# A decode step on one core: the last two rows of one weight matrix loaded in eight partition pieces, and repeated waits left out

## The chip, the cores and the metric

The kernel runs on one core of one Trainium2 chip. The metric is the device time of one execution in microseconds (us). Times come as the median of several runs; one more execution was taken with the hardware profiler, and all rows of the profile belong to that one.

## The reference

One token (a row of 1024 numbers) goes through an attention block over a long cache and through a small network beside it; the results are added. All inputs are bf16.

```
xn  = layernorm(A_x)                                     # 1 x 1024
q   = xn @ wq                                            # 32 heads of 128
o   = softmax(q k^T / sqrt(128)) v                       # 4 cached heads, 65536 positions each; 8 query heads share one
A   = o @ wo                                             # wo: 4096 x 1024
h   = gelu(layernorm(xn) @ w1), shifted by positions     # one position, so the shifts leave zeros
x1  = xn + h @ w2
B   = x1 + gelu(layernorm(x1) @ w3) @ w4                 # w3: 1024 x 3584, w4: 3584 x 1024
out = A_x + A + B
```

The caches are 2 x 4 x 65536 x 128 bf16, 128 MiB in all, and the weights about 36 MB; each byte is read once.

## The kernel before

Work is written out by hand into five queues, one for each engine (class `_Q`). A queue is a list of operations and of waits on semaphores; `emit` writes it out in that order, and the order in the list is the order on the engine. `_B` objects stand for buffers. Each keeps the events that wrote it (`w`) and those that read it (`r`) as a table from semaphore to value. Ahead of an operation, `_deps` puts a wait into the queue for every event that the buffers ask for; `_Q.wait` leaves out a wait whose value the same queue has already waited for. After it, `_done` records the operation's own event: `set_write` replaces the buffer's events, `add_write` (with `partial=True`) adds to them. TensorE's queue is rolled into a loop of eight passes of four tiles each (`emit_looped`), whose waits take their values from registers.

All large loads are issued by SyncE (SP), in one queue `q_sp`, through `_dma`. Each load has a semaphore of its own (`chan(name)`), which rises by 16 when the load has landed.

The stages are these. First `wq` (8 MB) and the first cache pieces are loaded, and the query is computed. Then come 32 tiles of 8192 positions (`NT`), the main loop. Each 4 MB load of keys or values serves two tiles; it goes into one of two slots of `KV`, and SP issues it when the readers of that slot (VectorE's transposes at L488 for keys, TensorE's products at L546 for values) are done with it. In the loop the tile's keys are transposed (L488), multiplied with the query (L499), turned into exponentials (L529), transposed back (L539), multiplied with the values (L546) and accumulated (L558, L560).

Late in the loop SP issues the loads of `w1`, `w2` and `w3`, then `wo` (8 MB, L629) into `KV`, then `w4` into the tile `WX`. `w4` is seen as 128 partitions of 28 rows; one row of one partition is 1024 bf16, 2 KB. It is loaded in three pieces of 20, 6 and 2 rows (`w4_parts`, L630), all 128 partitions at once, into column ranges of `WX` that do not overlap. Each piece has its own buffer object `b_W4[i]`, whose `r` is filled by hand at L632 to L636 with all earlier uses of that memory:

```
        w4_parts = [(0, 20), (20, 6), (26, 2)]
        b_W4 = [_B() for _ in w4_parts]
```

The last piece is 128 x 2 rows, so 4 KB for each partition and 512 KB in all. After the main loop TensorE does the products with `w1`, `w2`, `w3` (helper line L459) and with `wo` and `w4` (helper line L447). `w4_pe(i)` waits for piece i and issues four matmuls for each of its rows: 80, 24 and 8 of them. After the last eight VectorE copies the result out of PSUM (L664), and SP stores it, four partitions of 256 bf16 (L665); SP waits for that store, and the program ends.

Of the kernel before, what the change touches and what calls it, by code (L numbers as in the profile page):

```python
# [13 lines left out]
class _Q:  # L14
    def __init__(self, name, sem, in_order=False):
        self.name = name
        self.sem = sem
        self.in_order = in_order
        self.ops = []
        self.cnt = 0  # L20
        self.waited = {}
        self.marks = []
# [75 lines left out]
class _B:  # L98

    def __init__(self, name=""):  # L100
        self.name = name
        self.w = {}
        self.r = {}

    def set_write(self, ev):
        self.w = {ev[0]: ev[1]}
        self.r = {}

    def add_write(self, ev):
        self.w[ev[0]] = max(self.w.get(ev[0], 0), ev[1])  # L110

    def add_read(self, ev):
# [1 line left out]


def _deps(q, reads, writes):
    for b in reads:
        for s, v in b.w.items():
            q.wait((s, v))
    for b in writes:  # L120
        for s, v in list(b.w.items()) + list(b.r.items()):
            if not (q.in_order and s is q.sem):
                q.wait((s, v))


def _done(ev, reads, writes, partial=False):
    for b in reads:
        b.add_read(ev)
    for b in writes:
        if partial:  # L130
            b.add_write(ev)
        else:
            b.set_write(ev)


def _op(q, fn, reads=(), writes=(), partial=False):
    _deps(q, reads, writes)
    ev = q.op(fn, True)
    _done(ev, reads, writes, partial)
    return ev  # L140


def _grp(q, fns, reads=(), writes=(), partial=False):
    _deps(q, reads, writes)
    ev = None
    for i, fn in enumerate(fns):
        ev = q.op(fn, i == len(fns) - 1)
    _done(ev, reads, writes, partial)
    return ev
# [8 lines left out]
def _dma(q, chan, fn, reads=(), writes=(), partial=False):  # L158
    _deps(q, reads, writes)
    chan.n += 1  # L160
    ev = q.dma(fn, chan.sem, 16 * chan.n)
    _done(ev, reads, writes, partial)
    return ev


def bass_parallel_sum__gqa_block_cached__mixer_s_mlp__decode_kernel(
# [13 lines left out]
    P = 128  # L180
    D = A_x.shape[2]
# [15 lines left out]
    with ExitStack() as es:  # L197
        E = es.enter_context

        def sb(name, shape, dt):  # L200
            return E(nc.sbuf_tensor(name, shape, dt))
# [4 lines left out]
        def sem(name):  # L206
            return E(nc.semaphore(name))
# [52 lines left out]
        WX = sb("WX", [P, 14336 + 16384], BF)  # L260
# [23 lines left out]
        q_sp = _Q("sp", None)  # L284
# [3 lines left out]
        def chan(name):  # L288
            if name not in chans:
                chans[name] = _DmaChan(sem("d_" + name))  # L290
            return chans[name]
# [26 lines left out]
        def load_rows(dst, bufs, ch, w, r0, nrow):  # L318
            src = w.rearrange("(p r) n -> p (r n)", p=P)
            ncol = w.shape[1]  # L320
            _dma(q_sp, chan(ch), lambda e: e.dma_start(out=dst, in_=src[:, r0 * ncol:(r0 + nrow) * ncol]), writes=bufs)
# [309 lines left out]
        b_W4 = [_B() for _ in w4_parts]  # L631
        for i, (r0, nr) in enumerate(w4_parts):  # L632
            for b in [b_W, b_W2] + b_X[0] + b_X[1]:
                for d in (b.r, b.w):
                    for s, v in d.items():
                        b_W4[i].add_read((s, v))  # L636
            load_rows(WX[:, r0 * D:(r0 + nr) * D], [b_W4[i]], "w4%d" % i, B_w4, r0, nr)

        def w4_pe(i):
            r0, nr = w4_parts[i]  # L640
# [60 lines left out]
```

## Time and profile before

| | |
|---|---|
| median of 3 runs | 402.36 us (402.34 to 403.08) |
| the profiled execution's own time | 402.32 us |
| its span, first to last instruction | 401.1 us |
| outside the span | 1.2 us |
| moved from HBM | 169.87 MB, 424 GB/s over the span |
| busy: PE, DVE, ACT, POOL | 41%, 58%, 12%, 19% of the span |

The DMA engines (16 of them serve the core) are busy nearly all of the span; no compute engine is above 58%. The chain that ended last puts 64% of the span on DMA. SP issues the three pieces of `w4` at 349.97 to 351.25 us; their times from issue to landing are 43.7, 46.9 and 47.6 us. The last eight matmuls start at 398.51 us, and the result's store is issued at 399.40 us.

### The profile page before, as it was taken

Reading aid. Unit: us, or ns where it says so; the run is one execution under the profiler, and the core shown is the slowest. Engines: PE = TensorE matmul, PEld = TensorE weight load, DVE = VectorE, ACT = ScalarE, POOL = GpSimd, SP = SyncE. Lnnn points to the kernel's source line nnn. Section 1 sums busy time; section 2 is a strip of 40 time slices with the busy share of each in tenths; the row PEclk is TensorE's granted clock in tenths of the full one; section 3 lists DMA queues with packets and bytes.
Section 4 is the critical chain, followed back from the end, with each engine's and each line's share of the span. In section 5 each row is a group of like instructions: output and inputs, shape, how many; then the busy total and the mean of one; then the engine's idle time right before and its main releaser. Section 6 shows DMA issues by size and latency. Waiting matters only on the chain.

```text
span 401.1 us, 4292 instructions
## 1 busy us (share of the span) xinstructions
PE 165.6 (41%) x1544; PEld 53.3 (13%) x1560; DVE 231.8 (58%) x398; ACT 49.5 (12%) x132; POOL 77.1 (19%) x130
## 2 busy tenths in 40 slices
PE   0432325353443434343434343524353535536054
PEld 0211101011111111110111110101010101222032
DVE  0246566757575858585758585848585857354000
ACT  1000101111111111110202111111111112100000
POOL 5000003121223121112412121214112111420000
PEclk9985556556556565565565565565655655757567
DMA  8999999999999999999999999999999999999994
GB/s 356 428 418 435 446 422 422 451 433 418 431 449 428 422 448 432 425 428 444 431 422 448 435 425 428 444 429 422 451 431 425 428 448 408 473 443 440 414 395 181
DMA packets 6070, 170.03 MB, mean 424 GB/s; under 512 B 804, under 2 KB 808, under 8 KB 936
## 3 DMA queue, kind: packets, MB, share of 16 engines
q1 hardware_dynamic: 5912, 169.87, 98.3%
q8 instruction: 5, 0.08, 0.1%
q14 instruction: 9, 0.07, 0.0%
q10 hardware_dynamic: 144, 0.00, 0.0%
HBM read 169.87 MB, written 0.00 MB: 424 GB/s over the span
## 4 chain that ended last, share of the span: by engine, by line
DMA 64%; DVE 23%; PE 9%; ACT 2%; issue 1%; another core or an unknown queue 0%; SPq 0%; POOL 0%; ACTq 0%; DVEq 0%
DMA KV<-in_A_k_cache_dram 49%; DVE WX L488 14%; DMA WX<-in_B_w_dram 12%; PE S_ps L499 4%; DMA x_bf<-in_A_x_dram 3%; DVE pT_f L539 3%; DVE mrow L506 3%; ACT p_sb L529 2%; PE PT_ps L537 1%; PE MB_ps L512 1%; DVE Bst L516 1%; DVE Rm L507 1%; DVE brun L527 1%; PE MM_ps L459 1%; PE PT_ps L414 0%
## 5 line engine op out<-in xcount | busy, mean ns | idle before, releaser
L488 DVE STREAM_TRANSPOSE WX<-KV 128x1024 f32<-128x1024 f32 x128 | 151.9, 1217 | 65.3 <-DMA KV<-in_A_k_cache_dram 65.3
L546 PE MATMUL OT_ps<-KV,pT_f 128*32 128x512 bf16 x512 | 60.7, 627 | 56.3 <-DVE pT_f L539 55.5
L499 PE MATMUL S_ps<-WX,Ycur 128*32 128x512 bf16 x512 | 58.0, 599 | 17.6 <-DVE WX L488 17.3
L560 POOL TENSOR_TENSOR O_acc<-O_acc,tmpO 128x513 f32<-128x513 f32 x28 | 32.8, 1173 | 89.2 <-ACT tmpO L554 89.2
L558 POOL TENSOR_SCALAR O_acc<-O_acc,ff 128x513 f32<-128x513 f32 x28 | 19.6, 701 | 133.0 <-ACT ff L533 133.0
L529 ACT ACTIVATE p_sb<-S_ps,brun 128x512 bf16<-128x512 f32 x32 | 22.0, 688 | 170.3 <-DVE brun L527 143.4
L512 PE MATMUL MB_ps<-Rm,Lmat 128*128 128x16 bf16 x32 | 6.1, 192 | 86.1 <-DVE Rm L507 86.1
L554 ACT ACTIVATE tmpO<-OT_ps 128x512 f32<-128x512 f32 x32 | 19.2, 599 | 105.9 <-PE OT_ps L546 105.9
L506 DVE TENSOR_REDUCE mrow<-S_ps 128x1 f32<-128x512 f32 x32 | 21.6, 673 | 16.1 <-PE S_ps L499 16.1
L539 DVE STREAM_TRANSPOSE pT_f<-PT_ps 128x512 f32<-128x512 f32 x32 | 23.0, 717 | 6.3 <-PE PT_ps L537 4.4
L499 PEld LDWEIGHTS S_ps<-WX,Ycur 128*32 128x32 bf16 x512 | 14.4, 125 | 63.0 <-issue 33.4
L546 PEld LDWEIGHTS OT_ps<-KV,pT_f 128*32 128x32 bf16 x512 | 14.7, 129 | 58.4 <-DVE pT_f L539 29.8
L537 PE MATMUL PT_ps<-p_sb,permR 128*128 128x512 bf16 x16 | 9.5, 595 | 21.2 <-ACT p_sb L529 21.2
L512 PEld LDWEIGHTS MB_ps<-Rm,Lmat 128*128 128x128 bf16 x32 | 3.3, 102 | 112.3 <-DVE Rm L507 112.3
L664 DVE CAST orow<-OUT_ps 128x256 bf16<-128x256 f32 x1 | 0.4, 424 | 29.1 <-PE OUT_ps L447 29.1
L447 PE MATMUL OUT_ps<-KV,o_bf 128*1 128x256 bf16 x128 | 5.8, 368 | 14.5 <-DMA KV<-in_A_wo_dram 14.5
L516 DVE TENSOR_REDUCE Bst<-MB_ps 128x1 f32<-128x16 f32 x32 | 5.6, 175 | 9.2 <-PE MB_ps L512 9.2
L537 PEld LDWEIGHTS PT_ps<-p_sb,permR 128*128 128x128 bf16 x32 | 3.3, 103 | 45.2 <-ACT p_sb L529 45.2
L377 PE MATMUL MM_ps<-ln_s,ones_f 128*128 128x1 f32 x6 | 1.8, 362 | 17.3 <-DVE ln_s L376 17.3
L447 PE MATMUL OUT_ps<-WX,gh_bf 128*1 128x256 bf16 x112 | 4.8, 336 | 6.6 <-DMA WX<-in_B_w_dram 6.6
L389 POOL TENSOR_TENSOR ln_s<-ln_s,neghalf 128x1 f32<-128x1 f32 x3 | 1.7, 558 | 29.9 <-DVE ln_s L387 29.9
L556 POOL COPY O_acc<-tmpO 128x513 f32<-128x513 f32 x4 | 2.5, 619 | 24.0 <-ACT tmpO L554 24.0
(116 smaller groups left out, 113.5 us busy)
## 6 DMA issues: line engine op xcount, KB each, us to landing
KV<-in_A_k_cache_dram SPq DMA_DIRECT2D x16, 4096.0 KB, 23.5
KV<-in_A_v_cache_dram SPq DMA_DIRECT2D x16, 4096.0 KB, 22.0
KV<-in_A_wq_dram SPq DMA_DIRECT2D x2, 4096.0 KB, 16.7
KV<-in_B_w_dram SPq DMA_DIRECT2D x1, 7168.0 KB, 27.5
WX<-in_B_w_dram SPq DMA_DIRECT2D x1, 5120.0 KB, 43.7
WX<-in_B_w_dram SPq DMA_DIRECT2D x2, 2048.0 KB, 18.3
WX<-in_B_w_dram SPq DMA_DIRECT2D x1, 1536.0 KB, 46.9
WX<-in_B_w_dram SPq DMA_DIRECT2D x1, 512.0 KB, 47.6
```

What stands on the lines that cost most here:

```text
L447: fns.append(lambda e, lhs=lhs, rhs=rhs, jj=jj: e.matmul(OUT_ps[32 * jj:32 * jj + 1, 0:256], lhs, rhs[:, 256 * jj:256 * jj + 256], start=F ...
L488: _op(q_dve, lambda e, ix=ix: e.transpose(out=X32[:, xs, 1024 * ix:1024 * (ix + 1)], in_=KV32[:, 2 * s, 4096 * half + 1024 * ix:4096 * hal ...
L499: fns.append(lambda e, we=we, cm=cm, mv=mv: e.matmul(S_ps[32 * cm:32 * cm + 32, :], Ycur[:, we, :, :].rearrange("p a g -> p (a g)"), mv, s ...
L506: _op(q_dve, lambda e: e.reduce_max(mrow[:, m:m + 1], S_ps[:, :], axis=AX.X), reads=[b_S], writes=[b_mrow[m]])
L512: _op(q_pe, lambda e: e.matmul(MB_ps[:, 0:16], Lmat[:, :], Rm[:, m, :], start=True, stop=True), reads=[b_R[m], b_const], writes=[b_MB])
L529: _op(q_act, lambda e: e.activation(p_sb[:, m, :], S_ps[:, :], ACTF.Exp, bias=brun[:, kn:kn + 1], scale=SCALE, accum_out=tmpO[:, m, 512:513]),
L537: _op(q_pe, lambda e: e.matmul(PT_ps[:, :], permR[:, :], p_sb[:, m, :], start=True, stop=True), reads=[b_p[m], b_const], writes=[b_PT])
L539: _op(q_dve, lambda e: e.transpose(out=pT_f[:, :], in_=PT_ps[:, :]), reads=[b_PT], writes=[b_pT])
L546: fns.append(lambda e, q=q, q4=q4: e.matmul(OT_ps[32 * q4:32 * q4 + 32, :], pT_bf[:, q, :, 1], slot(1, s)[:, 8192 * half + 512 * q:8192 * ...
L554: _op(q_act, lambda e: e.activation(tmpO[:, m, 0:512], OT_ps[:, :], ACTF.Copy), reads=[b_OT], writes=[b_tmpO[m]], partial=True)
L558: _op(q_pool, lambda e: e.tensor_scalar(out=O_acc[:, :], in0=O_acc[:, :], scalar1=ff[:, m:m + 1], scalar2=0.0, op0=ALU.mult, op1=ALU.add), ...
L560: _op(q_pool, lambda e: e.tensor_tensor(out=O_acc[:, :], in0=O_acc[:, :], in1=tmpO[:, m, :], op=ALU.add), reads=[b_tmpO[m]], writes=[b_Oacc])
```

## The change

There are two edits. In the dependency code, `_deps` collects its waits in one table, `need`, with the largest value for each semaphore, and then asks for each once. A buffer also remembers in `whole` whether its last write replaced everything; if so, and if it has been read since, a new writer waits for the readers alone and no longer for the write that the readers had waited for.

In the loads, the third piece of `w4` is no longer one transfer of 128 partitions but eight transfers of 64, 15, 14, 12, 8, 6, 5 and 4 partitions (128 in all), each with a semaphore of its own and each written as a partial write of the same buffer object `b_W4[2]`. `w4_pe(2)` waits for all eight.

```
 def _deps(q, reads, writes):
+    need = {}
     for b in reads:
         for s, v in b.w.items():
-            q.wait((s, v))
+            need[s] = max(v, need.get(s, 0))
     for b in writes:
-        for s, v in list(b.w.items()) + list(b.r.items()):
+
+        for s, v in (list(b.r.items()) if b.r and b.whole else list(b.w.items()) + list(b.r.items())):
             if not (q.in_order and s is q.sem):
-                q.wait((s, v))
+                need[s] = max(v, need.get(s, 0))
+    for s, v in need.items():
+        q.wait((s, v))
...
     def set_write(self, ev):
         self.w = {ev[0]: ev[1]}
         self.r = {}
+        self.whole = True

     def add_write(self, ev):
+        self.whole = False
         self.w[ev[0]] = max(self.w.get(ev[0], 0), ev[1])
...
-            load_rows(WX[:, r0 * D:(r0 + nr) * D], [b_W4[i]], "w4%d" % i, B_w4, r0, nr)
+            if i < 2:
+                load_rows(WX[:, r0 * D:(r0 + nr) * D], [b_W4[i]], "w4%d" % i, B_w4, r0, nr)
+                continue
+            p0 = 0
+            for j, n in enumerate((64, 15, 14, 12, 8, 6, 5, 4)):
+                src = B_w4.rearrange("(p r) n -> p (r n)", p=P)[p0:p0 + n, r0 * D:(r0 + nr) * D]
+                _dma(q_sp, chan("w4%d%d" % (i, j)), lambda e, p0=p0, n=n, src=src: e.dma_start(out=WX[p0:p0 + n, r0 * D:(r0 + nr) * D], in_=src),
+                     writes=[b_W4[i]], partial=True)
+                p0 += n
+            assert p0 == P
```

More of the change, by code (lines that the diff above doesn't have):

```diff
@@ L107, in set_write @@
         self.r = {}
+        self.whole = True
     def add_write(self, ev):
+        self.whole = False
         self.w[ev[0]] = max(self.w.get(ev[0], 0), ev[1])
```

## The prediction

> **What bounds the kernel now.** I read the page's slices and chain first, then the table of stages, then the chain's last pieces, SP's own rows, and the tail in slices of half a microsecond. From the page, the slices of DMA and the chain:
>
> ```profile
> DMA  8999999999999999999999999999999999999994
> ...
> DMA 64%; DVE 23%; PE 9%; ACT 2%; issue 1%; another core or an unknown queue 0%; SPq 0%; POOL 0%; ACTq 0%; DVEq 0%
> ```
>
> No compute engine is full, while DMA is full in all but the ends. The stages (columns: window, its length, busy time of each engine, PE clock, DMA share, GB/s) say it more sharply:
>
> ```profile
> 20.00:100.00 80.00, 30.66 (x269) 9.27 (x268) 50.49 (x92) 9.42 (x25) 10.47 (x14) 0.61 1.00 432
> 100.00:200.00 100.00, 43.45 (x348) 11.37 (x345) 67.85 (x107) 14.89 (x41) 24.16 (x37) 0.55 1.00 433
> 200.00:300.00 100.00, 42.17 (x343) 11.58 (x353) 68.89 (x104) 15.36 (x43) 21.34 (x32) 0.57 1.00 432
> ```
>
> A DMA share of 1.00 at 432 GB/s means that the 16 engines never run dry in the loop; a 4 MB load takes 22 to 23.5 us from issue to landing but only 9.7 us of bandwidth, so more than one is always queued. The end is set by the last load, as the last pieces of the chain show (start, length, what):
>
> ```profile
> 350.82 47.64 DMA WX<-in_B_w_dram
> 398.46 0.04 issue
> 398.51 0.42 PE OUT_ps L447 x8
> 398.93 0.02 issue
> 398.95 0.42 DVE orow L664
> ```
>
> The piece of two rows, issued at 350.82, lands at 398.46; then eight matmuls, the copy and the store follow, 2.64 us to the span's end at 401.1. The tail in the same table:
>
> ```profile
> 395.50:396.00 0.50, 0.50 (x20) 0.31 (x12) 0.00 (x0) 0.00 (x0) 0.00 (x0) 0.50 0.42 172
> 396.00:396.50 0.50, 0.50 (x20) 0.35 (x16) 0.00 (x0) 0.00 (x0) 0.00 (x0) 0.66 0.14 57
> 396.50:397.00 0.50, 0.50 (x28) 0.42 (x20) 0.00 (x0) 0.00 (x0) 0.00 (x0) 1.00 0.02 8
> 397.00:397.50 0.50, 0.50 (x20) 0.20 (x16) 0.00 (x0) 0.00 (x0) 0.00 (x0) 1.00 0.08 33
> ```
>
> From 396.5 to 398.5 the four half-microseconds hold 8, 33, 25 and 33 GB/s, 25 in the mean, near 432/16 = 27: one of the 16 engines is late and finishes alone. That is what the change's odd sizes aim at.
>
> **Part 1, the split, if it were free.** One engine's share of the old piece is 512 KB/16 = 32 KB, 1.2 us at 27 GB/s. With 64 partitions it is 16 KB: 0.61 us less for the late engine. The first of the eight transfers then lands at 398.46 - 0.61 = 397.85. The other 256 KB would go to engines that are already idle.
>
> **Part 2, the wait that comes with it.** All eight transfers write one buffer object, `b_W4[2]`, as partial writes. A partial write adds its event to `w`, and `whole` is then false, so `_deps` makes each next transfer wait for every earlier one's event. SP is not marked in order, so nothing drops it. The instruction streams of the two kernels set side by side confirm it: the transfer of 64 has no new wait, that of 15 waits for the semaphore of the one of 64, that of 14 for the one of 15, and so on to the one of 4: seven new waits, each for a landing. SP now stands from about 351 us until 397.85, then issues one transfer, waits until it has landed, issues the next. Queued behind on SP are only the other pieces and the result's store, which waited for L664 anyway; but TensorE's last eight matmuls wait for all eight landings. So seven round trips of a small transfer stand one after another at the end, with all other work done: `w3` products, GELU and the first two `w4` pieces are over by 397.83. Nothing hides them.
>
> **The price of one round trip.** The trace has one small transfer on idle DMA engines, the result's store (SP's rows and SP's own waits: waiter <- releaser: us, times, longest):
>
> ```profile
> 349.97 1.28 SPq L321 DMA_DIRECT2D WX<-in_B_w_dram  x3
> 399.40 0.66 SPq L665 DMA_DIRECT2D out_dram<-orow  x1
> ```
> ```profile
> SPq L56 <- DMA out_dram<-orow: 1.0, 1, 1.0
> ```
>
> Issue 0.66, wait 1.0: 1.66 us. A piece differs in two ways. Each partition is 4 KB instead of 512 B: 0.15 us at 27 GB/s against 0.02, so +0.13. And 0.05 us passes from a landing to the next instruction (398.46 to 398.51). Sum 1.84.
>
> The other side is the first load at the start, on idle engines too, and like the pieces a read of HBM (first the issue, then the windows):
>
> ```profile
> 0.79 0.87 SPq L321 DMA_DIRECT2D KV<-in_A_wq_dram  x2
> ```
> ```profile
> 1.40:1.80 0.40, 0.00 (x0) 0.00 (x0) 0.06 (x1) 0.40 (x1) 0.40 (x5) 1.00 0.00 0
> 1.80:2.40 0.60, 0.00 (x0) 0.00 (x0) 0.00 (x0) 0.60 (x1) 0.60 (x4) 1.00 2.94 874
> 2.40:3.40 1.00, 0.00 (x0) 0.00 (x0) 0.00 (x0) 0.18 (x1) 0.70 (x6) 1.00 0.00 0
> 3.40:4.00 0.60, 0.00 (x0) 0.00 (x0) 0.00 (x0) 0.00 (x0) 0.60 (x3) 1.00 2.04 874
> 4.00:4.60 0.60, 0.00 (x0) 0.00 (x0) 0.00 (x0) 0.00 (x0) 0.60 (x2) 1.00 0.00 0
> 4.60:5.20 0.60, 0.00 (x0) 0.00 (x0) 0.00 (x0) 0.00 (x0) 0.60 (x3) 1.00 2.08 874
> ```
>
> Bytes are booked where a packet starts. The first wave starts 1.0 us after the issue; the second comes 1.6 us later, the third only 1.2 us after that, so a read on idle engines costs 0.4 more than a streamed one. The store's last packets start at 400.7 and it has landed at 401.06: 0.36. So 1.0 + 0.15 + 0.4 + 0.36 + 0.05 = 1.96. I take 1.9, between the two, as neither row is quite the case. Bounds: the store's row with the 0.33 us issue of the large loads instead of 0.66 gives 1.51; the load's sum with the store's longer issue (0.66 against the 0.40 of one `wq` load) gives 2.2.
>
> The Trainium skill, page "DMA: Bandwidth & Descriptors", section "Rules for kernel authors", speaks against this change: many small transfers should be merged, since under 64 KB one pays mostly overhead, and the seven are of 60 KB down to 16 KB. Its section "Anatomy of one DMA" puts the fixed part at about 2.0 us, fitted there for GpSimd's path; by that the seven would cost an estimated 14.0 us in place of 13.3.
>
> **Part 3, waits left out.** Against the old stream SP loses 34 waits that had long been reached (the old load into the same slot), TensorE six waits in each pass of its loop, GpSimd seven and VectorE six. A wait on SP takes 28 ns (median of 37), so SP saves 34 x 0.028 = 1 us spread over the kernel. I cost this at nothing: DMA is queued ahead at a share of 1.00, so an issue 0.03 us earlier moves no byte earlier. If that cover were gone, the most would be the 0.28 us of SP's longest wait; I keep 0.3 both ways.
>
> **Sum.** The last transfer lands at 397.85 + 7 x 1.9 = 411.15, against 398.46: +12.7. The tail of 2.64 us follows as before; were the clock granted to the eight matmuls halved by the pause, +0.4. Span 413.8, with the 1.2 us outside it 415.0. The profiled execution's 402.32 and the median of 402.36 are one number here. With the bounds: 402.32 - 0.61 + 7 x 1.51 - 0.3 = 412.0, and 402.32 - 0.61 + 7 x 2.2 + 0.4 + 0.3 = 417.8.
>
> **Rivals.**
>
> *Not slower: the eight are in flight together.* If each semaphore were reached before SP came to its wait, only the 0.61 us would remain: 401.7 us, which is within 0.2% of the old time (0.2%, 0.8 us, is about what a measurement here can tell from no change). For it: SP issues the first at 351 us and has 47 us to spare. Against it: the transfers queue behind 15 MB on the same engines, and SP reaches the first wait at 351, when its transfer has 47 us to go. It would decide below a round trip of 0.61/7 = 0.09 us, and the cheapest row says 1.5.
>
> *Slower still: an odd number of partitions falls on few engines.* Nothing in the trace shows a transfer of 15, 14 or 5 partitions. Were each run by one engine, row after row, 64 rows of 0.15 us take 9.6 us instead of 7 x 0.15 = 1.05: +8.5 on the sum, 423.5 us. For it: the late engine shows that work is tied to engines. Against it: the store's four partitions need no more than 0.1 us of packets. The same page's section "Why a DMA increments its semaphore by 16 and not by 1" says that the engine count is the largest number up to 16 that divides the partitions, so 15 engines for 15; no run here shows it.
>
> *Cheaper round trips only.* At 1.51 each, 412.3 us; that is inside the range.
>
> **How the numbers follow.** Serial round trips at 1.5 to 2.2: 0.91, predicted 415.0, range 412.0 to 417.8. In flight together: 0.03. Few engines: 0.04. Round trips outside my bounds: 0.02. Slower by over 0.2% is 0.96, within 0.2% is 0.03, faster by over 0.2% is 0.01 (in flight together, with all of the 0.3 us and some of the late engine's lag besides).
>
> **What would show it.** Right: SP's rows have one DMA issue each about 1.9 us from 397.9 on, eight of the short pieces in all; SP waits on its own transfers seven times; DMA is nearly empty from 398 to 411; the last eight matmuls start near 411.2; the loop's stages keep 432 GB/s and their length. Wrong: the eight issues stand together near 351 to 356 us; or the pieces of 15 and 14 take longer than those of 4 by more than 0.5 us; or the loop's stages change length by over 0.3 us.

## The result and the profile after

The changed kernel takes 416.74 us (median of 4 runs, 416.3 to 417.13) against 402.41 us before: a ratio of 1.0351, 95% interval 1.0338 to 1.0364. It is slower by 14.3 us. The forecast was 415.0 us, range 412.0 to 417.8. The profiled execution took 416.5 us with a span of 415.3 us, so again 1.2 us lie outside the span.

The loop did not move. The table of stages after (columns as before: window, length, busy time of PE, PEld, DVE, ACT, POOL, PE clock, DMA share, GB/s):

```profile
20.00:100.00 80.00, 33.26 (x264) 9.73 (x268) 50.59 (x92) 9.40 (x25) 10.49 (x14) 0.75 1.00 432
100.00:200.00 100.00, 45.96 (x353) 11.24 (x345) 67.85 (x106) 14.79 (x41) 23.88 (x37) 0.57 1.00 432
200.00:300.00 100.00, 46.70 (x353) 11.70 (x357) 69.34 (x104) 15.41 (x43) 21.35 (x32) 0.59 1.00 433
...
400.00:410.00 10.00, 0.00 (x0) 0.00 (x0) 0.00 (x0) 0.00 (x0) 0.00 (x0) 0.53 0.09 25
```

The DMA share is 1.00 at 432 GB/s as before, and PE's clock, 0.75 in one stage in place of 0.61, does not show in the rate. What is new is the last line: ten microseconds in which the core moves 25 GB/s and computes nothing. The end of the chain after (start, length, what) says what they are:

```profile
351.35 47.74 DMA WX<-in_B_w_dram
399.09 0.02 issue
399.11 1.99 DMA WX<-in_B_w_dram
401.09 0.02 issue
401.11 1.95 DMA WX<-in_B_w_dram
...
410.42 0.02 issue
410.44 1.88 DMA WX<-in_B_w_dram
412.32 0.14 issue
412.45 0.62 PE OUT_ps L454 x8
```

There are seven round trips, each from an issue on SP to the landing that SP waits for, end to end: 1.99, 1.95, 1.88, 1.88, 1.72, 1.82 and 1.88 us. With the pauses between them they reach from 399.09 to 412.32: 13.23 us, 1.89 each. SP's own waits (waiter <- releaser: us, times, longest):

```profile
SPq L650 <- DMA WX<-in_B_w_dram: 56.6, 7, 47.2
```

That is seven waits, of which the longest, 47.2 us, is for the piece of 64 behind the queue and was hidden; the other 9.4 us are the bare waits of the later trips, beside SP's issues.

### The profile page after: what moved, and what is told of

It reads as the page before. It is cut to its first block, busy times and chain, and to the rows that moved or that the text cites. A ratio compares the mean times of both kernels' runs of the same rounds, so it can differ in the third digit from the quotient of the medians.

```text
span 415.3 us, 4223 instructions
## 1 busy us (share of the span) xinstructions
PE 178.4 (43%) x1560; PEld 54.0 (13%) x1560; DVE 231.9 (56%) x398; ACT 49.5 (12%) x132; POOL 76.8 (18%) x130
## 4 chain that ended last, share of the span: by engine, by line
DMA 66%; DVE 20%; PE 9%; ACT 3%; issue 1%; SPq 0%; ACTq 0%
DMA KV<-in_A_k_cache_dram 49%; DMA WX<-in_B_w_dram 15%; DVE WX L495 12%; PE S_ps L506 4%; DVE pT_f L546 3%; DMA KV<-in_A_wq_dram 3%; ACT p_sb L536 3%; DVE mrow L513 3%; PE PT_ps L544 2%; PE MB_ps L519 1%; DVE Rm L514 1%; DVE Bst L523 1%; DVE brun L534 1%; PE MM_ps L466 1%; PE PT_ps L421 0%
## 5 line engine op out<-in xcount | busy, mean ns | idle before, releaser
L506 PE MATMUL S_ps<-WX,Ycur 128*32 128x512 bf16 x512 | 58.9, 607 | 17.9 <-DVE WX L495 17.5
L544 PE MATMUL PT_ps<-p_sb,permR 128*128 128x512 bf16 x32 | 18.4, 574 | 42.3 <-ACT p_sb L536 42.3
L421 PE MATMUL PT_ps<-KV,xn_bf 128*32 128x512 bf16 x32 | 5.1, 627 | 8.0 <-DMA KV<-in_A_wq_dram 8.0
```

Source lines behind the costliest of these rows:

```text
L506: fns.append(lambda e, we=we, cm=cm, mv=mv: e.matmul(S_ps[32 * cm:32 * cm + 32, :], Ycur[:, we, :, :].rearrange("p a g -> p (a g)"), mv, s ...
L544: _op(q_pe, lambda e: e.matmul(PT_ps[:, :], permR[:, :], p_sb[:, m, :], start=True, stop=True), reads=[b_p[m], b_const], writes=[b_PT])
```

## The experiments

The medians of before that stand beside these runs are those of the same chip.

**The waits away, the pieces kept.** Each piece gets a buffer object of its own; `w4_pe(2)` reads all eight.

```
+                b_own = _B()
+                b_own.r = dict(b_W4[i].r)
...
-                     writes=[b_W4[i]], partial=True)
+                     writes=[b_own], partial=True)
+                b_W4s.append(b_own)
```

> The changed kernel, with a buffer object of its own for each of the eight pieces, so that SP waits for none of them. Theory (seven serial round trips of 1.9 us): 13.3 us go, 416.7 becomes 403.4 if the first piece still lands 1.2 us later than I had it, 401.7 to 402.2 if it does not. Rival (pieces of odd size are slow in themselves): most of the 14 us stays, above 408 us.

Measured: 405.03 us against 402.79 (ratio 1.0057, 1.0044 to 1.0071). The waits are most of the loss, but 2.2 us stay, more than either branch of the theory. The end of TensorE in its timeline (start, length, engine, line, operation, then the idle time before it and its releaser):

```profile
393.79 4.44 PE L454 MATMUL OUT_ps<-WX,gh_bf 128*1 128x256 bf16 x80 [6.71 <-DMA WX<-in_B_w_dram]
399.33 0.83 PE L454 MATMUL OUT_ps<-WX,gh_bf 128*1 128x256 bf16 x24 [1.11 <-DMA WX<-in_B_w_dram]
401.19 0.39 PE L454 MATMUL OUT_ps<-WX,gh_bf 128*1 128x256 bf16 x8 [1.04 <-DMA WX<-in_B_w_dram]
```

The piece of six rows, which the change does not touch, lets its 24 matmuls start only at 399.33 (before, it had landed by 397.3), and the eight pieces are complete 1.8 us after that. So there are two costs here that the sum did not have: something slows the six-row piece, and something draws out the pieces behind it.

**The dependency code alone.** The split is undone, the new `_deps` kept.

> The changed dependency code alone; the last two rows load as one transfer of 128 partitions. Theory (pruned waits are hidden behind a full DMA queue): 402.4 us, within 0.3 of before, the last piece lands within 0.3 us of 398.5. Rival (the pruned waits shift the loop or the last issues, and so made the first piece land 1.2 us later than forecast): about 403.6 us.

Measured: 402.77 us against 402.79 (ratio 1.0002, 0.9993 to 1.0011). The last piece landed at 398.42, as before (398.46). The pruned waits are worth nothing that can be measured here, and are not what made the first piece late.

**Three round trips in place of seven.**

```
-            for j, n in enumerate((64, 15, 14, 12, 8, 6, 5, 4)):
+            for j, n in enumerate((64, 32, 16, 16)):
```

> The changed kernel with four pieces of 64, 32, 16 and 16 partitions, each still waiting for the one before: three round trips in place of seven. Theory (a fixed 1.9 us for each, with 0.15 more for the second row of each engine in the piece of 32): 416.7 - 4 x 1.9 + 0.15 = 409.3 us. Rival (odd sizes pay, even ones do not): a round trip of 1.5 us or less here, below 408.0 us.

Measured: 410.77 us (ratio 1.0203, 1.0187 to 1.0219). The trips, from its chain:

```profile
399.30 0.02 issue
399.32 2.31 DMA WX<-in_B_w_dram
401.63 0.02 issue
401.65 2.03 DMA WX<-in_B_w_dram
403.67 0.02 issue
403.69 2.07 DMA WX<-in_B_w_dram
```

The time is 1.5 us above the theory and 2.8 above the rival. Of the 1.5, 0.6 is in the trips (6.46 us from 399.30 to 405.76, against 5.85), and 0.4 is this chip's slower time before (402.79 against 402.41). Even sizes are not cheaper: the two of 16 take 2.03 and 2.07, while the pieces of 15 and 14 above took 1.99 and 1.95, and those of 4 to 8 took 1.72 to 1.88. The piece of 32 pays 0.26 more than one of 16 instead of the 0.15 that I had set.

**The split without the new dependency code.**

> The dependency code of before, with the eight serial pieces. Theory (the pruned waits are worth nothing): 416.7 us, within 0.4. Rival (the pruned waits cost the 1.2 us by which the first piece was late): 415.5 us.

Measured: 417.48 us against 402.79 (ratio 1.0371, 1.0355 to 1.0387). This is 0.8 above the theory, outside its 0.4, and further from the rival; 0.4 of it is again this chip's time before. The interval of the ratio overlaps that of the changed kernel. In the profiled execution the first piece landed at 399.75, 0.66 later than in the changed kernel, and the seven trips took 13.18 us (2.04, 1.96, 1.89, 1.83, 1.69, 1.80 and 1.85), as there. Both halves of the edit are now priced: the pruning nothing that can be measured, the split everything.

**Why the six-row piece is slow.** In the traces of before and of the dependency code alone, no 12 KB packet of that piece took more than 465 ns. After the change, and with the pieces in flight, many took 600 to 1250 ns, and these begin at about 393.5 us, when the first engines have reached the piece of 64 (its first packets start at 393.3 to 393.4) while others still work on the six rows. Four kernels with two pieces of 64 in flight cross the two sides, SBUF and HBM. The edit replaces the eight slices by pairs of (partitions of SBUF, rows of HBM); written short here, `lo` and `hi` are the halves, `ev` and `od` every second one:

```
+            for j, (dp, sp_) in enumerate(((ev, ev), (od, od))):     # even and odd
+            for j, (dp, sp_) in enumerate(((lo, lo), (hi, hi))):     # halves
+            for j, (dp, sp_) in enumerate(((lo, ev), (hi, od))):     # halves in SBUF only
+            for j, (dp, sp_) in enumerate(((ev, lo), (od, hi))):     # halves in HBM only
```

> Two pieces in flight, the even partitions and then the odd ones, each with its own buffer object. The question is why the 6-row piece, whose packets took 460 ns in every engine before, has packets of 600 to 1250 ns as soon as a 64-partition piece follows it. Theory A (64 neighbouring partitions of SBUF are too narrow a target for 16 engines): no slow packets here, 402.8 us as before. Theory B (64 neighbouring rows of HBM are too narrow a source): the same, 402.8 us. Theory C (any split disturbs the row of engines): slow packets, 403.9 to 404.3 us.

> Two pieces in flight, partitions 0 to 63 and 64 to 127. The late engine again carries eight rows, as in the kernel before. Theories A, B and C alike: slow packets, the 6-row piece lands about 1.3 us late, 403.9 to 404.3 us. If instead the odd small pieces did it, 402.8 us.

> Two pieces in flight: the even rows of HBM into partitions 0 to 63, the odd rows into 64 to 127. This changes the order of the rows of the last matrix's last piece, so that part of the result is another one. SBUF as in the halves, HBM as in the even and odd. Theory A (SBUF): slow packets, 403.9 to 404.3 us. Theory B (HBM): 402.8 us.

> Two pieces in flight: rows 0 to 63 of HBM into the even partitions, rows 64 to 127 into the odd ones; this too changes the order of the rows of that piece and so a part of the result. HBM as in the halves, SBUF as in the even and odd. Theory A (SBUF): 402.8 us. Theory B (HBM): slow packets, 403.9 to 404.3 us.

Measured, against 402.67 us:

| pieces | us | ratio, 95% interval |
|---|---|---|
| even and odd in both | 402.73 | 1.0005, 0.9996 to 1.0014 |
| halves in both | 404.5 | 1.0046, 1.0033 to 1.0059 |
| halves in SBUF, even and odd in HBM | 404.5 | 1.0047, 1.0033 to 1.0062 |
| even and odd in SBUF, halves in HBM | 402.87 | 1.0007, 0.9997 to 1.0016 |

The loss goes with SBUF and not with HBM: theory A, and 0.2 us more than it had set. In the same order the six-row piece landed at 397.15, 399.84, 399.39 and 397.22 us (before: 397.26), and its longest packet took 465, 1226, 1249 and 465 ns. One line of each one's stage table, in the same order, shows it too:

```profile
394.00:395.00 1.00, 1.00 (x24) 0.63 (x20) 0.00 (x0) 0.00 (x0) 0.00 (x0) 0.50 0.84 344
```
```profile
394.00:395.00 1.00, 0.98 (x20) 0.65 (x24) 0.00 (x0) 0.00 (x0) 0.00 (x0) 0.50 1.12 221
```
```profile
394.00:395.00 1.00, 1.00 (x24) 0.65 (x20) 0.00 (x0) 0.00 (x0) 0.00 (x0) 0.50 1.04 164
```
```profile
394.00:395.00 1.00, 1.00 (x27) 0.68 (x20) 0.00 (x0) 0.00 (x0) 0.00 (x0) 0.50 0.82 340
```

The DMA share is the second number from the end, GB/s the last. Where the target is spread, 0.82 to 0.84 of the engines' time moves 340 GB/s; where it is 64 neighbouring partitions, more of their time moves half to two thirds of that. The engines are occupied, not idle, and what slows them goes with the target in SBUF.

The Trainium skill, page "DMA: Bandwidth & Descriptors", section "The descriptor swizzle", offers a reason: in a 128-partition transfer each of the 16 engines writes a port of its own, and partitions 0 to 63 have only half of the ports. The runs show the effect and its side; the ports themselves no run shows. The same page's section "Rules for kernel authors" says of two transfers to disjoint halves that they take turns on the same engines, and advises one of 128 partitions; the advice holds here, and the two halves cost 1.8 us more (404.5 against 402.67).

**The pieces spread in SBUF.** The changed kernel's sizes, but 64 even partitions first and the other sizes among the odd ones; once with the waits away, once with them.

```
+                o = 2 * p0 if j == 0 else 2 * p0 - 127
+                sl = slice(o, o + 2 * n - 1, 2)
```

> The eight pieces in flight with the changed kernel's sizes, but each takes every second partition (64 even ones, then 15, 14, 12, 8, 6, 5 and 4 odd ones), so that no piece is narrow in SBUF except the last few. Theory (what was left of e1_in_flight is two things: 1.8 us from the narrow piece of 64, and a late engine that is one of the first four and so gets 4 + 7 = 11 rows in place of 8): 403.2 us, 0.5 above before, with one engine alone at the end. Rival (the late engine is among the last, as the sizes suppose, and gets 4 rows): 402.1 us. Second rival (many small pieces cost by themselves even in flight): 404 us or more.

Measured: 404.55 us against 402.45 (ratio 1.0041, 1.0028 to 1.0055), 1.3 above the theory and in the range of the second rival. The span does not support that rival: it is 402.5 us, 1.3 more than the 401.2 that this chip mostly shows for before, so 2.1 us of the profiled execution's 404.6 lie outside it in place of 1.2, for a reason that stays open. Inside the span, the first branch of the theory holds only in part: the six-row piece landed at 397.94, 0.7 late, and a few of its packets still took up to 862 ns. This points to the small pieces behind it, as with the piece of 64 alone behind it (the next run) none of its packets after 391 us took more than 465 ns; how they do it was not tried. After the piece of 64, at 398.56, the seven others land at 398.74, 398.92, 399.11, 399.30, 399.49, 399.67 and 399.85, one every 0.18 us. Its windows (the DMA share and GB/s last) show how little moves meanwhile:

```profile
398.00:399.60 1.60, 0.81 (x24) 0.46 (x24) 0.00 (x0) 0.00 (x0) 0.00 (x0) 1.00 0.05 18
```

18 GB/s over 1.6 us is 29 KB, seven rows of 4 KB. That is one engine, alone, with one row of each piece: in the trace these packets follow one another without overlap, and those of all other engines had ended by 397.0. So the first rival is out: the late engine belongs to the four that even the piece of 4 uses, and the sizes give it eleven rows in place of eight, 3 x 0.16 = 0.5 us more. The kernel with the eight pieces as neighbours in flight ends in the same way, with four rows and then seven single ones.

> The changed kernel with its seven waits as they are, each piece taking every second partition. Theory (the first piece was late only because its 64 partitions are neighbours): it lands near 397.9 in place of 399.1, the seven round trips stay at 1.9 us, and the sum of the prediction comes out: 415.0 to 415.6 us. Rival (the wait of SP itself delays the first piece): 416.7 us.

Measured: 417.98 us (ratio 1.0382, 1.0366 to 1.0398). The first pieces of its chain:

```profile
351.26 46.77 DMA WX<-in_B_w_dram
398.03 0.02 issue
398.05 2.46 DMA WX<-in_B_w_dram
```

The first piece lands at 398.03, within 0.2 of the theory, and the six-row piece 3.63 us after the one before it, as in the kernel before (3.64); so the late start of the changed kernel was the narrow target. The total misses it, for a reason of its own: the round trips are now 2.25 us in the mean ((413.77 - 398.03)/7). SP's DMA instructions, by their line (min/median/max ns), here and in the changed kernel:

```profile
L652 SPq DMA_DIRECT2D WX<-in_B_w_dram x8: 577/690/947, 351.3 to 411.7; - x8
```
```profile
L650 SPq DMA_DIRECT2D WX<-in_B_w_dram x8: 248/285/567, 351.4 to 410.4; - x8
```

A step of two in the partitions makes the issue 0.4 us longer, about the difference between 2.25 and 1.89. A transfer that nobody waits for hides this; a chain pays it seven times.

## Why the prediction was right, and by how much not

The mechanism was right: seven waits of SP on its own transfers, seven trips end to end. By its terms, against the profiled execution:

- **The round trips**: 7 x 1.9 = 13.3 forecast, 13.23 measured. The store at the end and the cold first load, the two rows between which it was taken, gave 1.84 and 1.96. The 14.0 that I had estimated from the Trainium skill ("DMA: Bandwidth & Descriptors", "Anatomy of one DMA") was further off. That the sum came out to 0.01 a trip is in part luck, as two errors cancel: I let the store's long issue of 0.66 us stand for these, but theirs is 0.29, and their wait for the landing is 9.4/6 = 1.57 us in place of 1.13.
- **The gain of 0.61 on the first landing** was the mis-sized term. The piece landed at 399.09, not at 397.85. Part 1 took it that half the rows are half the time, and that whatever stood ahead in the queue would not notice. The first held: the late engine's last packets, four in place of eight, took 0.62 us in place of 1.24. The second did not: the six-row piece landed at 398.61, 4.71 us after the one before it; before the change it was 3.64. The crossed halves, and the serial pieces spread in SBUF, put this on 64 neighbouring partitions as a target. The stream ahead was also 0.3 late already.
- **The tail** of 2.64 measured 2.93: the matmuls took 0.62 in place of 0.42 with the clock at 0.50, 0.20 of the 0.4 that was allowed for, and 0.14 instead of 0.04 passed before the first of them. These 0.10 were not in the sum. The prediction also has the products of the first two `w4` pieces end at 397.83; that is the end of their weight loads, and the matmuls ran to 398.12. Nothing hung on it here, as the trips outlast both.
- **The pruned waits** at nothing: shown within the interval of 0.1%, by 402.77 against 402.79.
- **Summed up**: +1.24, -0.07 and +0.29 make 1.46, which is the span's 415.26 less the 413.8 forecast.

Of the rivals, *in flight together* was set at 401.7 us; the kernel that really is in flight takes 405.03. So the change would have lost even without the waits, and my reading that its sizes favour the late engine took the intention for the effect. *Few engines* is out: the piece of 15 took 1.99, and one engine with 15 rows would have needed 2.3 for its packets alone. The profile of the changed kernel also counts 868 packets under 512 B in place of 804, 64 more, and in the trace these are 4-byte writes, one for each partition of the seven small pieces. What the Trainium skill says of the number of engines ("DMA: Bandwidth & Descriptors", "Why a DMA increments its semaphore by 16 and not by 1") fits this.

No version here beats the kernel before. The last piece as one transfer of 128 partitions, or as even and odd ones in flight, comes out the same. The late engine is not all that bounds the end there. Before, TensorE stood for only 0.38 us ahead of the last eight matmuls, so an earlier last piece could have saved about 0.4 us, an estimate from that gap, and not the whole 0.61. In the profiled executions of the dependency code alone and of the even and odd targets there is no gap at all: TensorE's clock stayed at 0.50 to 398 us, where before it had been back at 1.00 from 396.5, and the chain goes through its products, as with the dependency code alone:

```profile
393.62 5.50 PE OUT_ps L454 x107
```

Why the one engine is late was not tried.

## What to carry to other kernels

When a transfer is cut, look first at what its pieces share in the dependency code: partial writes of one buffer object can make the queue wait for each landing, and a small landing that nothing hides cost 1.9 us here. Before trying to balance engines by choosing sizes, find out which engine is late and which engines the small transfers use; here every small piece went to the late one too. Look also at what else ends there; here a perfect split had about 0.4 us to gain. If a load must be cut, let each piece still spread over all partitions, and remember that a piece which is narrow in SBUF also slows its neighbours in the queue.

## What the runs showed of the hardware that was not expected

- Two transfers to 64 neighbouring partitions each are slower than one to 128 of the same bytes, by 1.8 us for 512 KB at the end of a full queue; the loss goes with the target in SBUF, and most of it falls on the piece ahead. Two of 64 even and 64 odd partitions cost nothing (402.73 against 402.67).
- A transfer with a step of two in its partitions takes SP 0.69 us to issue in place of 0.29.
- A round trip does not depend on whether the number of partitions is odd. At 4 KB for each partition it took 2.31 us for 32, 1.95 to 2.07 for 14 to 16, 1.83 to 1.89 for 8 and 12, 1.69 and 1.72 for 6, and again 1.80 to 1.88 for 4 and 5, over the three kernels whose pieces are neighbouring partitions and wait for one another.
